# Reordered steps, four places for raw weights, and two fold copies on another engine in a fused recurrence and Fourier-mixing kernel

## Chip, cores and metric

The kernel runs on one core of a Trainium2 chip. The metric is the time of one execution on the device in microseconds; lower is better. Five engines run side by side, each in the order in which its instructions were written: TensorE (PE, matrix products), VectorE (DVE), ScalarE (ACT), GpSimd (POOL) and SyncE (SP, which here only issues DMAs). They wait for one another by semaphores.

## What is computed

Two blocks follow one another. The first is a gated recurrence over 768 tokens, for 4 batches and 8 heads of dimension 48:

```
f = 1 / (1 + exp(-f_logit))
for t in range(S):
    state = f[:, :, t, :, None] * state + einsum('bhd,bhe->bhde', k[:, :, t], v[:, :, t])
    y[:, :, t] = einsum('bhd,bhde->bhe', q[:, :, t], state)
```

The heads are laid side by side, which gives x of 768 tokens by 384 channels for each batch. The second block mixes it by a two-dimensional Fourier transform and then runs a two-layer network:

```
mixed = real(fft(fft(x, axis=1), axis=2))
u  = x + mixed
un = (u - mean(u)) / sqrt(var(u) + 1e-6)
out = u + relu(un @ w_ch1) @ w_ch2        # 384 -> 1536 -> 384
```

## The kernel before

Work is cut into steps, and a hand-written list of words, `ORDER`, says in which order the steps are issued. A loop walks over the list and calls a generator or a function for each word. Nothing else sets the order: each engine gets its share of every step in the order of the list, and waits where an operand is not there yet.

**Attention units.** A number (0 to 15) is the next step of one unit; a unit is two heads of one batch, so units 0 to 3 make batch 0. In the text, 1.7 is step 7 of unit 1. The steps: 0, ScalarE turns the logits into log gates (L372, L373); 1, VectorE scans them (L379, L380); 2, ScalarE takes three exponentials (L383 to L387); 3, VectorE multiplies them into q and k (L391, L392); 4, PE makes the scores inside blocks of 64 tokens (L400); 5, VectorE masks them (L404); 6, PE makes the first half of the values and the scores across blocks, ScalarE copies these; 7, PE makes the rest of the values (L559) and the state products (L599); 8, VectorE scans the states (L607); 9, PE adds what the states give (L616), ScalarE empties the accumulator `y` in five copies; 10, PE turns the result into token rows (L636) and ScalarE copies them to `x`; 11, the fold, on VectorE, which adds and subtracts token tiles in mirror pairs for the transform (L663 to L669); 12, for the last two units of a batch, a second fold along the channels (L678 to L687). `y` exists once, so the values of one unit start after the copies of the unit before.

`K3` turns the keys of unit 3 (PE, then a ScalarE copy). `L3fk` has SP issue the loads of f and k of unit 3; q, k and f are 344 KB each, in two DMAs, v is 369 KB. The homes of f, k and q are few and are reused by later units, so a load can wait until an earlier unit has read its own.

**Weights.** The weights come as 64-bit words. `r` fetches one raw block of 393 KB (24 in all), `R` three, and `C` makes 32-bit floats of one block (ScalarE L281, VectorE L283 and L284, POOL L285). Raw blocks take turns in a pool of three buffers, so a fetch waits for the block three before it. `V` and `c` read weight blocks a second time, late in the run, to judge their size (L344); `M` decides from that whether everything has to be done again in another way, which doesn't happen with these inputs.

**Mixing and network.** `F1` is the next step of batch 1's transform: four products with tables into `z`, which ScalarE copies, and three mixing steps, each of which adds to two token tiles of `x`. `H1` is the next step of the normalisation of batch 1: moments of a tile, or a tile normalised by VectorE (L779), turned by PE (L782) and copied by ScalarE. `P1` is the next step of the network for batch 1, which takes pairs of token tiles. For batches 1 to 3 the first layer is a scheme of 15 products (`PRODUCTS`, L840), each with sums of tokens made by VectorE before it (L814), an evacuation by ScalarE (L847) or an addition by VectorE (L849), and a ReLU by ScalarE (L851). The second layer is a scheme of seven products (L894) into two accumulators. `B` makes sums of weights for the first scheme, `W` for the second.

**Pairs and stores.** `PAIRS` names the pairs of token tiles, `LAST_PAIRS` those of the last batch: (2, 5), (1, 3), (0, 4). A tile's rows go back to the output as soon as they are finished: tiles 1, 2, 3 and 5 by an indirect DMA on POOL's queue (L692), tile 0 by one DMA and tile 4 by three on SP's queue. The last pair of the last batch, (0, 4), has a branch of its own (L915 to L933): its products come in another order, so that after the last one only half a tile (192 columns) is left to add and store.

**Spare products.** `D` calls `busy()`, which issues eight products of 128 by 128 bf16 constants into an unused corner of `y`. They compute nothing that is used. The list holds 21 `D`.

`T` loads the tables, `S` sorts them (POOL), `Z` and `I` set constants (POOL), and `i` loads an identity matrix.

Of the kernel before, what the change touches and what calls it, by code (L numbers as in the profile page):

```python
# [27 lines left out]
    "L0f Z I 0 L0q L2q D D L1f L0k D 0 D 0 i D 1 L2f 2 0 D D D L0v 0 L1k K0 D 0 0 D L1q 0 1 D r 1 L3fk D "  # L28
    "D D L1v 2 0 L2k 1 D r r D 1 2 1 3 3 0 C K1 1 2 0 C 1 L3q 2 1 3 C L2v 2 r K2 L4fk 3 L3v L5fk 1 2 1 D "
    "T 2 0 4 3 D C S 1 2 5 3 D 2 3 2 4 K3 3 D L5qv L4qv 5 4 3 2 3 L6fk 3 2 3 5 R 3 F0 F0 4 6 F0 L6qv F0 C "  # L30
    "C 4 C 5 4 F0 r 5 K4 D 4 H0 r 4 r H0 C H0 4 C r L7fk F0 6 4 P0 C P0 6 5 P0 7 C F0 4 P0 r K5 r C L7qv "
    "P0 P0 r r 5 6 C 6 5 r 7 C 5 P0 r 7 P0 C P0 5 r 7 K6 C P0 6 C P0 r r 6 7 7 C C 6 6 r 5 P0 P0 r C 6 r "
    "C K7 H0 r P0 C 7 L9fk 6 H0 L8fk P0 L8qv C B 7 C H0 B 7 B 9 9 B 8 P0 8 9 P0 P0 L9qv P0 6 8 P0 P0 P0 "
    "P0 9 P0 P0 8 7 B 9 K9 P0 P0 5 P0 B 6 P0 P0 B P0 7 W P0 9 B H0 9 8 9 B H0 7 P0 L11fk P0 11 P0 P0 P0 "
    "P0 P0 P0 4 11 9 P0 P0 P0 P0 P0 9 B P0 P0 P0 P0 7 L11qv P0 8 11 F1 P0 8 K8 F1 F1 11 F1 L10fk 8 8 10 "
    "F1 P0 8 11 H1 L10qv B 10 F1 P0 B P0 B P0 11 P0 P0 10 B 10 H1 P0 10 K10 P0 B 10 H1 10 K11 L12fk P1 P1 "
    "P1 P1 P1 P1 P1 B P1 P1 P1 P1 P0 P1 P1 P1 F1 P1 P1 H1 10 9 12 10 P1 P1 12 10 9 8 P1 P1 P1 L12qv 12 11 "
    "12 12 8 11 P1 L13fk 12 11 H1 10 H1 P1 11 H1 H1 P1 P1 P1 P1 P1 P1 P1 P1 P1 P1 P1 P1 P1 P1 10 P1 P1 12 "
    "K12 10 P1 12 L13qv 11 P1 L14fk 12 11 P1 13 13 12 P1 P1 11 P1 14 13 P1 F2 P1 14 F2 P1 P1 P1 P1 P1 P1 "
    "P1 P1 P1 P1 P1 14 P1 13 F2 P1 L14qv 14 P1 F2 13 13 F2 13 K13 F2 14 13 H2 F2 13 14 H2 P1 L15fk P1 P1 "  # L40
    "15 15 13 K14 P1 P1 L15qv P1 14 P1 H2 14 H2 H2 P2 14 P2 P2 15 P2 P2 P1 P2 P2 P2 15 V P2 P2 P2 P2 P2 "
    "P2 P2 13 14 15 H2 H2 15 K15 15 13 12 15 14 P2 15 14 15 P2 P2 V c 12 P2 15 P2 c V 14 P2 15 P2 H2 P2 "
    "P2 P2 15 c F3 F3 F3 P2 V V P2 P2 P2 c V c P2 V P2 c P2 P2 V P2 F3 c P2 P2 V F3 F3 P2 F3 H3 P2 P2 P2 "
    "P2 P2 P2 P2 P2 H3 P2 V P2 P2 V H3 P2 P2 c P2 P2 V P2 c c P2 P2 P2 V P2 P2 P2 P2 P2 P2 P2 c P2 P2 V "
    "P2 H3 V P2 P2 H3 P3 H3 c P3 P3 c P3 P3 c P3 P3 P3 P3 c V P3 V P2 P3 P3 P3 c P3 P3 P3 P3 P3 V V P3 P3 "
    "P3 P3 V H3 P3 P3 P3 H3 P3 c P3 P3 P3 P3 c P3 P3 P3 P3 P3 V P3 P3 P3 P3 P3 P3 P3 P3 c P3 P3 P3 P3 P3 "
    "V P3 P3 c P3 V P3 c P3 c P3 P3 V c c P3 P3 P3 P3 P3 P3 M P3 P3 P3 P3 P3 P3 P3 P3"
# [32 lines left out]
LAST_PAIRS = ((2, 5), (1, 3), (0, 4))  # L80
# [3 lines left out]
def kernel(  # L84
# [81 lines left out]
    small = fixed([128, 2 * NF], "small")  # L166

# [21 lines left out]
    def busy():  # L189

        for _ in range(8):
            nc.tensor.matmul(spare, lhsT=bound[:, :C], rhs=bound[:, :C], start=not started, stop=True,  # L192
                             skip_group_check=True)
            started.append(True)
# [111 lines left out]
    def words(i):  # L306
        _, src, cols = blocks_of[i]
        raw = pr.tile([128, 2, 3, DM // 2], U32, tag="raw", name=f"raw{i}").rearrange("p a b n -> p (a b n)")
# [380 lines left out]
    def store(b, c, rows):  # L689
# [7 lines left out]
        for i, j, o in {0: [(0, C, 0)], 4: [(0, 1, 3 * QS), (1, 16, HS + 1), (16, C, HS + 16)]}[c]:  # L697
            nc.sync.dma_start(out=out[b, o:o + j - i], in_=rows[i:j])
# [155 lines left out]
    def projected(b, x, again=False):  # L854
# [5 lines left out]
        for j, (c, d) in enumerate(PAIRS if b < B - 1 else LAST_PAIRS):  # L860
            if again:
                for _ in range((3, 3, 2)[j]):
                    next(behind[b], None)
# [250 lines left out]
```

## Time and profile before

| | |
|---|---|
| runs before | 524.42, 525.7, 527.98 us, median 525.7 |
| profiled execution | 527.98 us, of which the profile's span is 526.3 |
| PE busy | 494.9 us, 94% of the span |
| VectorE busy | 378.3 us, 72% |
| ScalarE busy | 218.4 us, 42% |
| POOL busy | 58.8 us, 11% |
| mean granted PE clock | 0.974 of full speed |
| first product of batch 0's transform | 59.54 us |
| last product ends | 519.43 us |
| DMA | 48.15 MB, 91 GB/s on average |

Busy time is the time in which an engine has at least one instruction running; the span is from the first instruction of the profiled execution to the last. Some 1.7 us of the execution lie outside the span. A busy share over the whole span is an average of stages with different limits, so it has to be read together with the view that cuts the span into stretches. In the profile a group of instructions is named by the line of the kernel, the engine and the operation; "idle before" tells how long the engine stood still just before an instruction and what released it.

### The profile page before, as it was taken

The numbers are of one execution on the slowest core, as the hardware profiler recorded it, in microseconds if no ns is written. First come the engines' busy times: TensorE is split into PE (matmuls) and PEld (weight loads), VectorE is DVE, ScalarE is ACT, GpSimd is POOL, SyncE is SP. The second block draws the span as 40 slices with busy tenths as digits, with TensorE's granted clock in tenths as the row PEclk, the third lists the DMA queues.
The fourth block names the chain that finished last, engine by engine and source line by source line (L and its number), as shares of the span: only waits on it lengthen the run. The fifth ranks groups of instructions, "written<-read, shape, count | busy, mean of one in ns | idle before, by whom it ended". The sixth has DMA issues, their size and how long they took to land.

```text
span 526.3 us, 13807 instructions
## 1 busy us (share of the span) xinstructions
PE 494.9 (94%) x5854; PEld 453.4 (86%) x5854; DVE 378.3 (72%) x746; ACT 218.4 (42%) x520; POOL 58.8 (11%) x85
## 2 busy tenths in 40 slices
PE   5878599999999999999999999999999999999994
PEld 4757388866899889999999999999999999999994
DVE  3598989989955368688588776779776667465571
ACT  5567368656331542453435523550431404031220
POOL 3045033551001000000001000000001000010100
PEclk9789699999999999999999999999999999999998
DMA  8957837575010230103212012120610312220200
GB/s 222 268 147 206 210 109 214 161 221 158 6 55 30 68 97 17 54 21 114 77 55 84 1 55 72 46 63 23 206 43 15 107 47 81 83 91 8 84 11 27
DMA packets 20650, 48.15 MB, mean 91 GB/s; under 512 B 3426, under 2 KB 6179, under 8 KB 20579
## 3 DMA queue, kind: packets, MB, share of 16 engines
q1 hardware_dynamic: 19474, 43.63, 29.5%
q0 software_dynamic: 1104, 3.54, 1.8%
q8 instruction: 48, 0.79, 0.6%
q14 instruction: 24, 0.19, 0.1%
HBM read 42.44 MB, written 4.72 MB: 90 GB/s over the span
## 4 chain that ended last, share of the span: by engine, by line
PE 87%; DVE 6%; issue 2%; ACT 2%; DMA 1%; POOL 0%; SPq 0%; DVEq 0%; ACTq 0%
PE ub L840 23%; PE fx L894 16%; PE fz L894 11%; PE up L871 9%; PE z L724 5%; PE y L559 4%; PE mix L743 3%; PE y L616 2%; PE sc L400 2%; PE ds L599 2%; PE po L880 2%; PE yt L636 2%; PE pt L782 1%; PE st L538 1%; PE y L192 1%
## 5 line engine op out<-in xcount | busy, mean ns | idle before, releaser
L849 DVE TENSOR_TENSOR h<-h,ub 128x512 f32<-128x512 f32 x81 | 55.2, 687 | 33.5 <-PE ub L840 24.5
L692 POOL DMA_INDIRECT out_dram<-x,place x16 | 16.4, 1024 | 357.6 <-DVE x L944 224.3
L847 ACT ACTIVATE h<-ub 128x512 f32<-128x512 f32 x54 | 31.9, 591 | 42.3 <-PE ub L840 42.3
L871 PE MATMUL up<-unT,w 128*128 128x256 f32 x216 | 49.4, 382 | 0.0
L840 PE MATMUL ub<-wide,w 128*128 128x128 f32 x360 | 45.0, 276 | 2.3 <-DVE wide L814 2.3
L894 PE MATMUL fx<-block,h 128*128 128x192 f32 x264 | 46.9, 328 | 0.0
L894 PE MATMUL fx<-w,h 128*128 128x192 f32 x264 | 45.5, 327 | 0.0
L840 PEld LDWEIGHTS ub<-wide,w 128*128 128x128 f32 x360 | 42.4, 192 | 3.4 <-PE pt L782 1.3
L871 PEld LDWEIGHTS up<-unT,w 128*128 128x128 f32 x216 | 40.1, 190 | 5.9 <-ACT h L873 0.4
L851 ACT ACTIVATE h<-h 128x512 f32<-128x512 f32 x45 | 28.4, 631 | 38.1 <-DVE h L849 37.7
L894 PEld LDWEIGHTS fx<-block,h 128*128 128x128 f32 x264 | 43.2, 190 | 0.5 <-DVE x L911 0.2
L894 PEld LDWEIGHTS fx<-w,h 128*128 128x128 f32 x264 | 42.7, 190 | 0.4 <-issue 0.2
L285 POOL TENSOR_TENSOR w<-w,raw 128x384 uint32<-128x384 uint32 x24 | 29.4, 1228 | 72.3 <-DVE w L284 39.1
L840 PE MATMUL ub<-unT,w 128*128 128x128 f32 x288 | 37.0, 275 | 0.0
L840 PEld LDWEIGHTS ub<-unT,w 128*128 128x128 f32 x288 | 34.6, 192 | 0.0
L783 ACT COPY unT<-pt 128x384 f32<-128x384 f32 x24 | 11.4, 484 | 46.8 <-PE pt L782 46.6
L840 PE MATMUL ub<-unT,wide 128*128 128x128 f32 x216 | 29.1, 278 | 0.0
L840 PE MATMUL ub<-wide 128*128 128x128 f32 x216 | 28.6, 275 | 0.1
L873 ACT ACTIVATE h<-up 128x256 f32<-128x256 f32 x36 | 13.9, 385 | 33.6 <-PE up L871 22.0
L840 PEld LDWEIGHTS ub<-unT,wide 128*128 128x128 f32 x216 | 26.4, 192 | 0.5
L840 PEld LDWEIGHTS ub<-wide 128*128 128x128 f32 x216 | 26.3, 192 | 0.3 <-PE ub L840 0.3
L379 DVE TENSOR_TENSOR_SCAN W<-g,bound 112x768 f32<-112x768 f32 x12 | 21.0, 1747 | 6.7 <-ACT g L373 6.7
(194 smaller groups left out, 1000.1 us busy)
## 6 DMA issues: line engine op xcount, KB each, us to landing
raw<-in_w_ch_dram SPq DMA_DIRECT2D x24, 384.0 KB, 5.1
v<-in_v_dram SPq DMA_DIRECT2D x16, 288.0 KB
k<-in_w_ch_dram SPq DMA_DIRECT2D x12, 384.0 KB, 3.4
g<-in_w_ch_dram SPq DMA_DIRECT2D x12, 384.0 KB, 3.3
k<-in_qkf_dram SPq DMA_DIRECT2D x14, 288.0 KB
g<-in_qkf_dram SPq DMA_DIRECT2D x12, 288.0 KB, 3.5
q<-in_qkf_dram SPq DMA_DIRECT2D x12, 288.0 KB, 3.3
wide<-in_qkf_dram SPq DMA_DIRECT2D x10, 288.0 KB, 4.7
```

Of the source, the lines that this page charges most:

```text
L285: nc.gpsimd.tensor_tensor(bits, bits, lo, ALU.add)
L379: nc.vector.tensor_tensor_scan(W, g, bound[:R], 0.0, ALU.add, ALU.min)
L559: nc.tensor.matmul(y[FILL[g], c // 3, c % 3 * C + t.start:c % 3 * C + t.stop], lhsT=vals[rows, o:o + (64 if g == 0 else D)], rhs=weights, ...
L692: nc.gpsimd.indirect_dma_start(out=out.rearrange("b s d -> (b s) d"), out_offset=bass.IndirectOffsetOnAxis(ap=place[:, b, i:i + 1], axis=0 ...
L724: nc.tensor.matmul(z[:, cols], lhsT=src[:, j, lo:hi], rhs=tab[:, t, T % 2, cols], start=(i == 0), stop=(i == len(parts) - 1), skip_group_c ...
L743: nc.tensor.matmul(mix[:, o], lhsT=zz[:rows_of[T], T, PLACES[c]], rhs=cd[:rows_of[T], T, :NQ - odd], start=(i == 0), stop=(i == 1))
L840: nc.tensor.matmul(chains[chain][:, m * 128:(m + 1) * 128], lhsT=block(w)[:, m * 128:(m + 1) * 128], rhs=tokens(a), start=(new and m == 0) ...
L847: nc.scalar.activation(out, got, kind, scale=1.0 if how == "=+" else -1.0)
L849: nc.vector.tensor_tensor(out, out, got, ALU.add if how == "+" else ALU.subtract)
L851: nc.scalar.activation(out, out, AF.Relu)
L871: nc.tensor.matmul(pp[:, :256], lhsT=w1[:, kt, m * 128:(m + 1) * 128], rhs=unT[:, kt], start=(kt == 0), stop=(kt == 2))
L894: nc.tensor.matmul(out, lhsT=h[:, m], rhs=blocks[i][:, m], start=(start and m == 0), stop=(m == H - 1), skip_group_check=True)
```

## The change

Six things change.

1. `busy()` issues two products instead of eight. The same constants are read as 32-bit floats, 128 of them. A 32-bit product is recorded by the profile as two products with two weight loads.
2. The raw weight blocks get a fixed tile, `ring`, with four places used in turn, instead of a pool of three. The three temporary blocks of `combine()` lie in it too.
3. In the fold, the two copies between VectorE's additions and subtractions (L667 and L668) are issued on ScalarE.
4. The pairs of the last batch are (2, 5), (1, 4), (3, 0), normalised in that order.
5. The branch for the last pair goes; the last pair runs as every other pair does. Tile 0 of the last batch is stored on ScalarE's DMA queue.
6. `ORDER` is another list, of the same 720 words: every word occurs as often as before.

```diff
-    "L0f Z I 0 L0q L2q D D L1f L0k D 0 D 0 i D 1 L2f 2 0 D D D L0v 0 L1k K0 D 0 0 D L1q 0 1 D r 1 L3fk D "
-    "D D L1v 2 0 L2k 1 D r r D 1 2 1 3 3 0 C K1 1 2 0 C 1 L3q 2 1 3 C L2v 2 r K2 L4fk 3 L3v L5fk 1 2 1 D "
-    "T 2 0 4 3 D C S 1 2 5 3 D 2 3 2 4 K3 3 D L5qv L4qv 5 4 3 2 3 L6fk 3 2 3 5 R 3 F0 F0 4 6 F0 L6qv F0 C "
-    "C 4 C 5 4 F0 r 5 K4 D 4 H0 r 4 r H0 C H0 4 C r L7fk F0 6 4 P0 C P0 6 5 P0 7 C F0 4 P0 r K5 r C L7qv "
...
+    "L2q Z I L0f D D L1f i 0 D L2f L0k D L0q D D L1k 1 D L0v D D 0 D 2 L3q D 0 0 1 D 0 K0 1 0 D 0 L1q 1 r "
+    "L3fk D 1 L2v L2k 3 2 C 1 0 L1v r 0 D 2 D 0 K1 2 K2 3 1 1 L5fk L3v 2 L4fk C 1 T 2 3 3 1 r 5 1 D r D 5 "
+    "2 4 3 S 1 2 D L6fk 2 3 4 2 0 K3 3 L5qv 0 D 3 3 2 3 C 2 3 3 2 5 3 D 4 F0 6 5 F0 L4qv F0 R F0 C L6qv 4 "
+    "C 4 C 4 F0 4 L7fk K4 4 C H0 H0 4 K5 4 H0 6 L7qv 6 F0 r P0 r 6 C r r 5 5 4 C L8fk P0 7 P0 P0 r 5 6 C "
...
-LAST_PAIRS = ((2, 5), (1, 3), (0, 4))
+LAST_PAIRS = ((2, 5), (1, 4), (3, 0))
...
+    ring = fixed([128, 3 * NF // 2 * HD], "ring")
...
-        for _ in range(8):
-            nc.tensor.matmul(spare, lhsT=bound[:, :C], rhs=bound[:, :C], start=not started, stop=True,
-                             skip_group_check=True)
+        words = bound.bitcast(F32)[:, :C]
+        for _ in range(2):
+            nc.tensor.matmul(spare, lhsT=words, rhs=words, start=not started, stop=True, skip_group_check=True)
...
-        raw = pr.tile([128, 2, 3, DM // 2], U32, tag="raw", name=f"raw{i}").rearrange("p a b n -> p (a b n)")
-        raw = raw[:, :768].rearrange("p (n w) -> p n w", w=2)
+        raw = ring[:, i % 4 * 2 * DM:(i % 4 + 1) * 2 * DM].bitcast(U32).rearrange("p (n w) -> p n w", w=2)
...
-        nc.vector.tensor_copy(f[:, 1:7:5], f[:, 0:8:7])
-        nc.vector.tensor_copy(f[0:1, 0], f[0:1, 2])
+        nc.scalar.copy(f[:, 1:7:5], f[:, 0:8:7])
+        nc.scalar.copy(f[0:1, 0], f[0:1, 2])
         tt(f[0:1, 2:7:4], x[0:1, 0:2, ch], x[0:1, 3:5, ch], ALU.subtract)
...
-            nc.sync.dma_start(out=out[b, o:o + j - i], in_=rows[i:j])
+            queue = nc.scalar if (b, c) == (B - 1, 0) else nc.sync
+            queue.dma_start(out=out[b, o:o + j - i], in_=rows[i:j])
...
-            if (b, c) == (B - 1, 0):
-                nc.sync.dma_start(out=out[b, :C, :HD], in_=c1)
...
-                tt(c2, Z, c2, ALU.add)
-                nc.sync.dma_start(out=out[b, :C, HD:], in_=c2)
```

In the new list unit 2's q is the first load, ahead of unit 0's f; all three first steps of units 0, 1 and 2 stand ahead of unit 0's exponentials (0.2); twelve `D` stand ahead of unit 0's scores (0.4), and the runs of `D` behind them are shorter; all 21 `D` stand ahead of batch 0's transform, where before one stood behind it. The late part of the list, from batch 1's network on, has the same words in a similar order.

## The prediction

> **What bounds the kernel now.** The page comes first. TensorE (PE) is busy for 494.9 of 526.3 us, so the digits by slice must say where it is not.
>
> ```profile
> PE 494.9 (94%) x5854; PEld 453.4 (86%) x5854; DVE 378.3 (72%) x746; ACT 218.4 (42%) x520; POOL 58.8 (11%) x85
> ...
> PE   5878599999999999999999999999999999999994
> ...
> DVE  3598989989955368688588776779776667465571
> ...
> PEclk9789699999999999999999999999999999999998
> ```
>
> Each digit is 13.2 us. PE is below 9 in the first five slices and in the last, and its clock is down in the same early slices. Next comes the table of stretches.
>
> ```profile
> 15.00:20.00 5.00, 2.68 (x72) 2.12 (x69) 2.34 (x4) 3.85 (x6) 0.00 (x0) 0.77 1.05 274
> 20.00:25.00 5.00, 5.00 (x54) 4.80 (x52) 2.57 (x3) 2.17 (x4) 0.00 (x0) 0.55 1.03 290
> 25.00:30.00 5.00, 4.35 (x161) 3.72 (x164) 3.97 (x6) 2.98 (x10) 0.04 (x1) 1.00 0.28 63
> ...
> 26.00:58.00 32.00, 22.63 (x595) 18.67 (x587) 29.38 (x53) 21.51 (x53) 13.35 (x20) 0.85 0.74 189
> 58.00:145.00 87.00, 83.97 (x1094) 66.07 (x1095) 79.55 (x134) 51.09 (x130) 25.73 (x21) 0.96 0.52 148
> 145.00:519.00 374.00, 370.71 (x3822) 352.62 (x3820) 257.85 (x548) 130.56 (x314) 14.87 (x15) 1.00 0.20 60
> ```
>
> The columns are PE, weight loads, VectorE (DVE), ScalarE (ACT), POOL, the granted clock, the DMA share and GB/s. There are three stages. From 0 to 26 us everything waits, behind loads (DMA share 1.05) and a PE at half clock. From 26 to 58 VectorE is busy 29.4 of 32 us and is the bound. From 58 PE is: 84.0 of 87, then 370.7 of 374. So PE's work after the first transform is fixed, and the end moves with the moment that F0 (batch 0's transform) starts, with PE idle time after it (1.5 us of the 3.0 up to 145, and 3.3), and with the last 7 us. The timeline shows how VectorE lost the first stage and what releases F0:
>
> ```profile
> 18.33 0.48 PE L559 MATMUL y<-at,v 64*48 64x64 f32 x7 [2.25 <-issue]
> 20.11 4.93 PE L192 MATMUL y<-bound 128*128 128x128 bf16 x48
> ...
> 20.23 0.76 DVE L607 TENSOR_TENSOR_SCAN stt<-ds,te 112x288 f32<-112x288 f32 x1 [2.82 <-PE ds L599]
> ...
> 25.96 1.04 DVE L404 COPY_PREDICATED at<-causal,sc 128x768 f32<-128x768 uint32 x1 [3.08 <-PE sc L400]
> ...
> 58.98 0.46 DVE L681 TENSOR_TENSOR se<-xs 128x285 f32<-128x285 f32 x1
> ...
> 59.54 2.85 PE L724 MATMUL z<-tab,se 128*95 128x385 f32 x6 [4.38 <-issue]
> ```
>
> PE stopped 2.25 us on nothing that the profile names, in the middle of unit 0's values; the trace has a 16 KB instruction packet running from 15.73 to 16.93, so I read it as code arriving late. Then six D steps (48 spare products) ran at half clock, 4.93 us, ahead of unit 1's scores, and VectorE waited 2.82 and 3.08 us. At the end of the stage PE waited 4.38 us for `se` (58.98 + 0.46 = 59.44), and F0 began at 59.54.
>
> **The front, old sum.** I add VectorE's rows by step: scan 1.92, the two products 1.94, mask 1.03, state scan 0.75, fold 2.47, second fold 1.0 or 3.2, a weight block 1.1. Up to F0 the old list holds 44.8 us of it, 2.3 of that after `se`: 42.5 before it. Idle before VectorE's steps: 6.48 + 0.97 + 1.20 + 2.82 + 3.08 = 14.55, then 1.35 + 0.20. 42.5 + 16.1 = 58.6 against 59.4; the 0.8 more is rows stretched here (1.27 for a weight row of 0.56, 0.90 for a copy of 0.20). I keep it as 0.9.
>
> **The front, new list.** Loads in the old trace land at some 255 GB/s, 1.35 us for each of 344 KB, the first at 4.5, and 2.13 MB at 11.56. L2q now stands ahead of L0f, so f0 lands at 5.9 and unit 0's two ScalarE passes (1.9) end at 7.8: VectorE starts 1.3 later than 6.48. Its scan ends at 9.75. ScalarE now has units 1 and 2's passes ahead of unit 0's exponentials: 7.8 to 9.7, and 9.7 to 11.6 (f2, 1.44 MB, is in by 8.8), so the first exponential ends at 12.45, where it was 9.38. q0 completes 2.13 MB, 11.5. VectorE waits 2.7 there; idle so far is 10.5. From there it has work queued: 0.3, 1.1, 0.5 at 16.3, 1.3 at 17.95 (q1 in at 17.0), 2.1, a weight block, 1.5, 0.8 at 23.85, 2.3 at 24.6 (k2 in at 24.0), 3.1. The twelve D steps ahead of unit 0's scores last at most 12 x 0.82 = 9.8 us (half clock, 4.93/6 each) from 4.6, that is to 14.4, when those scores are ready anyway. No later useful step has more than two D directly before it. Later waits by the same walk: 1.2 for unit 1's states (its values wait until 27.4 for ScalarE to empty `y`), 1.35 for f5's passes, 0.9 for unit 2's rows.
>
> VectorE's work to F0 is 43.7 us by the same rows (one weight block fewer), less 2.3 after `se`, less four times the two copies (0.26 + 0.24): 39.4. **The copies on ScalarE** don't free VectorE as much as they take off it: L669 writes rows that the copies read and write, so it must wait for both. Rows nearest to them are ScalarE's copies of 265 and 180 ns; with two handovers of about 0.1 that is 0.7 of waiting for 0.5 of work, if ScalarE is free. Lower bound -0.5 (hidden wholly); upper bound 2.0, behind one product of 0.89 and one activation of 0.63. I take 0.7, since up to F0 ScalarE is busy only 21.5 of 32 us. Sum: 39.4 + 0.9 + 10.5 + 1.2 + 1.35 + 0.9 + 4 x 0.7 = 57.0, so F0 at 57.1: **-2.5 us**. Bounds: -4.5, if q2 costs f0 only its two issue slots (0.93) and the later waits vanish; +1.5, if loads lag by a further 1 us (the old trace's lag grows from 1.15 to 2.2 us by 19.06), the code stall comes back on the path (2.25 less 1.2 of slack) and two later waits grow by 1 each. PE's useful work before F0 is the same in both lists, so the shift passes on whole.
>
> **D in float words.** Eight bf16 products become two f32 ones, each recorded as two. The row ub<-wide gives 0.89 us for eight such records at full clock, so a D is 0.45; bf16 measured 0.53 to 0.62. Cost nothing before F0, where D fills idle time; uncovered it would be 21 x 0.45. The one D that stood behind F0 (before unit 4's values) is now ahead: **-0.45**. PE instructions of a D fall from 16 records to 8, 168 in all, some 13% of the first 1,280; that makes late code less likely, and I book nothing for it.
>
> **Raw words in four places.** In the old trace SP stands at a raw load from 23.5 to 31.5 until a place is free, all loads behind it: hence 63 GB/s above. With four places and the new list SP first stands at L5fk, for unit 1's last read, about 28.3. VectorE's queue hides that: 0 in the sum. After F0, raw data made VectorE wait 0.76 at 109 and 0.96 at 116.6; near the end of the weights the new list is tighter (the last fetch five steps ahead of its use, thirteen before), so 0, from -1 to +1.5.
>
> **Later folds and pair changes.** Twelve folds follow F0, some with ScalarE queued behind PE's products. VectorE has 7.5 us spare in 58 to 145 and over 100 after. Where PE needs VectorE two products later, a wait of 2.0 less 2 x 0.89 leaves PE 0.22 us each, at most 2.6 in all; the lower end is -0.6, half of the two gaps of 0.69 and 0.57 at 100.7 and 117.5. I take **+0.8**, a little under the middle, for the spare time. At the change of pairs (0.52, 0.61, 0.94 us) both lists put the same filler within two steps: 0, from -1 to +1.
>
> **The end.**
>
> ```profile
> 517.52 0.56 DVE L927 TENSOR_TENSOR x<-fx,x 128x384 f32<-128x384 f32 x1 [1.59 <-PE fx L894]
> ...
> 519.47 0.36 DVE L930 TENSOR_TENSOR x<-fz,x 128x192 f32<-128x192 f32 x1 [1.39 <-PE fz L894]
> 519.86 0.36 SPq L931 DMA_DIRECT2D out_dram<-x  x1
> ```
>
> The branch for the last pair goes. After the last product there is now the 384-column addition, 0.56 for 0.36, then one issue on ScalarE's queue, which has nothing before it: **+0.2**. The indirect store of tile 3 is ready one product (1.95) earlier and takes POOL 1.02, so it lies under that. Four issues on SP become none.
>
> **Sum.** -2.5 - 0.45 + 0.8 + 0.2 = -1.95. The profiled execution took 527.98, 2.3 above the median of 525.7, so it becomes 526.0 and the median **523.7**.
>
> [...] PE's clock in the trace is 1.0 from 7.4 to 17.7, half to 24.5, full to 34.7, half to 41.6, and half again from 55.2 to 65.5. In the stretch 14.26 to 17.68 PE was busy for 1.8 of 3.4 us, and the clock fell at its end: half a stretch of idling was enough. The new list leaves PE some 5 us idle just before F0 with one D in it, so the clock falls there again. F0's 28 products at half clock took 8.4 us where a later batch takes 5.2: 3.1 us lost now and, in my sum, lost again. [...]
>
> **Rivals.** *VectorE waits for ScalarE in the folds.* L669 then waits 2.0, not 0.7, because ScalarE takes its queue in order. Four folds ahead of F0 cost 4 x 1.3 = 5.2 more: F0 at 62.3, sum +3.25, **528.9**, slower than before. It decides once the wait passes 0.7 + 1.95/4 = 1.2 us. For it: ScalarE is the engine between PE and VectorE all through these units. Against it: its 10 us of idle time in 26 to 58. *The front's gain is given back*, in lost cover behind F0: folds at 2.6 instead of 0.8 and pair changes at their +1 give 2.8 more, **526.5**. For it: PE's own gaps there are short because VectorE is just in time. Against it: VectorE's share drops. *The clock stays up.* If spare products spread singly keep every window over half full, F0's 3.1 us and some 1.5 of the units' slow steps go too: **519.1**. Against it: the 5 us gap before F0. *The edits do nothing that can be seen*, since the front's order is bound by loads: 525.7; it lies between the others and shares the second one's chance.
>
> **How the numbers follow.** Forecast 0.48 (own range 521 to 526), gain given back or no effect 0.24, folds waiting 0.16, clock kept 0.12. Leaving out the tails of the outer two gives 518.0 to 530.5. One per cent, 5.3 us, is about what a measurement of this kernel can tell from no change: faster than 520.4 takes the clock's case and a little of the forecast's edge, 0.14; slower than 531.0 takes half of the folds' case, 0.09; within, 0.77.
>
> **What would show it.** VectorE's first scan at 7.8, not 6.48; its idle time before the 16th microsecond larger, and no wait of 2.8 or 3.1 between 17 and 26; F0's first product near 57; L669 some 0.7 us after the end of L666; full DMA between 26 and 28 us; the clock half around F0; PE continuous after it, ending near 517.3. F0 at 59.5 or later, or PE gaps of over 8 us after F0, would prove it wrong.

## The result, and the profile after

The changed kernel takes 531.29 us (median of 20 runs, 528.69 to 534.44); the kernel before took 525.92 in the same rounds. The ratio is 1.0096, with a 95% interval of 1.0074 to 1.0118: about 1% slower, where 523.7 was forecast. The profiled execution took 533.2 us, its span is 531.5, 5.2 longer than before.

The page of the changed kernel, its busy times and its slices of 13.3 us:

```profile
PE 494.9 (93%) x5770; PEld 453.6 (85%) x5770; DVE 371.5 (70%) x714; ACT 226.6 (43%) x552; POOL 57.0 (11%) x85
...
PE   5787599899999999999999999999999999999994
```

PE is busy for exactly as long as before, 494.9 us, so the 5.2 us are PE idle time. The digits differ from before in slices two to four and in the eighth, which was a 9 and is an 8. The table of stretches (PE, weight loads, VectorE, ScalarE, POOL, clock, DMA share, GB/s) says which stages hold them:

```profile
20.00:25.00 5.00, 3.95 (x132) 3.54 (x136) 4.92 (x8) 4.28 (x7) 1.02 (x1) 1.00 1.04 231
25.00:30.00 5.00, 3.75 (x116) 3.00 (x116) 4.05 (x6) 3.41 (x11) 0.00 (x0) 1.00 0.27 71
26.00:58.00 32.00, 21.98 (x562) 18.60 (x560) 21.05 (x37) 18.14 (x52) 8.81 (x18) 0.87 0.79 212
58.00:145.00 87.00, 81.17 (x1080) 63.86 (x1081) 78.46 (x126) 56.59 (x142) 25.49 (x22) 0.95 0.50 143
145.00:519.00 374.00, 368.61 (x3795) 349.63 (x3794) 255.98 (x532) 135.87 (x334) 15.90 (x14) 1.00 0.20 60
```

The start went as forecast: from 20 to 25 us VectorE is busy for 4.92 of 5, where it was busy for 2.57, and the waits of 2.82 and 3.08 us near 20 and 26 are gone. Then the gain goes. From 26 to 58 VectorE is busy for 21.05 of 32 us, before for 29.38: it is no longer the engine that works through, it waits. From 58 to 145 PE works 2.80 us less than before, from 145 on 2.10 less. The timeline of the changed kernel shows the waits of the first stage (start, duration, engine, line; the bracket is the idle time before and what ended it):

```profile
39.28 0.36 DVE L666 TENSOR_TENSOR eo<-eo 128x192 f32<-128x192 f32 x1
40.20 0.84 ACT L372 ACTIVATE g<-g 112x768 f32<-112x768 f32 x1 [2.60 <-DMA g<-in_qkf_dram]
...
41.91 0.34 ACT L667 COPY eo<-eo 128x192 f32<-128x192 f32 x1
42.28 0.27 ACT L668 COPY eo<-eo 1x96 f32<-1x96 f32 x1
42.58 0.34 DVE L669 TENSOR_TENSOR eo<-x 1x192 f32<-1x192 f32 x1 [2.94 <-ACT eo L668]
...
50.06 0.35 DVE L669 TENSOR_TENSOR eo<-x 1x192 f32<-1x192 f32 x1 [1.08 <-ACT eo L668]
55.44 0.73 DVE L669 TENSOR_TENSOR eo<-x 1x192 f32<-1x192 f32 x1 [0.81 <-ACT eo L668]
58.41 0.35 DVE L669 TENSOR_TENSOR eo<-x 1x192 f32<-1x192 f32 x1 [0.72 <-ACT eo L668]
...
60.55 2.85 PE L725 MATMUL z<-tab,se 128*95 128x385 f32 x6 [4.93 <-issue]
```

VectorE finished L666 at 39.64 and could not go on before 42.58. The two copies take 0.34 and 0.27 us, but ScalarE stood until 40.20 at unit 4's first step (4.0), for unit 4's f, did its two passes, and only then came to the copies. The four folds ahead of F0 wait 2.94 + 1.08 + 0.81 + 0.72 = 5.55 us. F0 starts at 60.55, 1.0 later than before. Behind it PE idles 8.66 us up to its last product, before 4.77: that is 1.0 + 3.9 of the 5.2. PE's busy time behind F0 grew by another 0.4 (455.5 us, before 455.1). The end, from PE's last product to the end of the span, is as long as before (6.80 for 6.82):

```profile
523.40 0.97 POOL L692 DMA_INDIRECT out_dram<-x,place  x1 [28.72 <-DVE x L925]
524.72 0.56 DVE L929 TENSOR_TENSOR x<-fx,x 128x384 f32<-128x384 f32 x1 [1.59 <-PE fx L895]
526.55 0.38 ACTq L699 DMA_DIRECT2D out_dram<-x  x1
```

### The profile page after: what moved, and what is told of

Its sections match the earlier page's. It is cut to its first block, busy times and chain, and to the rows that moved or that the text cites. A ratio compares the mean times of both kernels' runs of the same rounds, so it can differ in the third digit from the quotient of the medians.

```text
span 531.5 us, 13640 instructions
## 1 busy us (share of the span) xinstructions
PE 494.9 (93%) x5770; PEld 453.6 (85%) x5770; DVE 371.5 (70%) x714; ACT 226.6 (43%) x552; POOL 57.0 (11%) x85
## 4 chain that ended last, share of the span: by engine, by line
PE 79%; DVE 8%; DMA 6%; ACT 3%; issue 2%; SPq 1%; DVEq 0%; ACTq 0%
PE ub L841 23%; PE fx L895 16%; PE fz L895 12%; PE up L872 5%; PE z L725 5%; PE y L559 3%; PE po L881 3%; PE mix L744 2%; DMA g<-in_qkf_dram 2%; DMA wide<-in_qkf_dram 2%; PE y L616 2%; PE ds L599 2%; PE pt L783 2%; DVE w L285 1%; PE yt L636 1%
## 5 line engine op out<-in xcount | busy, mean ns | idle before, releaser
L692 POOL DMA_INDIRECT out_dram<-x,place x16 | 18.4, 1148 | 384.7 <-DVE x L925 252.3
L895 PE MATMUL fx<-ring,h 128*128 128x192 f32 x264 | 46.6, 327 | 0.0
L872 PEld LDWEIGHTS up<-unT,w 128*128 128x128 f32 x216 | 40.2, 190 | 6.3 <-ACT h L874 0.8
L895 PEld LDWEIGHTS fx<-ring,h 128*128 128x128 f32 x264 | 43.3, 190 | 0.1
L286 POOL TENSOR_TENSOR w<-w,ring 128x384 uint32<-128x384 uint32 x24 | 27.0, 1131 | 70.3 <-ACT ring L282 30.2
L770 ACT ACTIVATE rstd<-mv,eps 128x1 f32<-128x1 f32 (+1 forms) x20 | 5.9, 294 | 43.1 <-DVE mv L767 43.1
```

What stands on the lines that cost most here:

```text
L286: nc.gpsimd.tensor_tensor(bits, bits, lo, ALU.add)
L692: nc.gpsimd.indirect_dma_start(out=out.rearrange("b s d -> (b s) d"), out_offset=bass.IndirectOffsetOnAxis(ap=place[:, b, i:i + 1], axis=0 ...
L872: nc.tensor.matmul(pp[:, :256], lhsT=w1[:, kt, m * 128:(m + 1) * 128], rhs=unT[:, kt], start=(kt == 0), stop=(kt == 2))
L895: nc.tensor.matmul(out, lhsT=h[:, m], rhs=blocks[i][:, m], start=(start and m == 0), stop=(m == H - 1), skip_group_check=True)
```

## The experiments

All eighteen in one table. F0, PE's idle time from F0 to its last product, and the tail (last product to the end of the span) are from each kernel's one profiled execution; ratios are to the kernel before in the same rounds (median 525.8 to 526.5).

| run | what it is | median us | ratio, 95% interval | profiled us | F0 at | PE idle behind F0 | tail |
|---|---|---|---|---|---|---|---|
| before | | 526.2 | | 527.98 | 59.54 | 4.77 | 6.82 |
| after | | 531.29 | 1.0096 [1.0074, 1.0118] | 533.2 | 60.55 | 8.66 | 6.80 |
| e1 | after, copies on VectorE | 529.3 | 1.0058 [1.0036, 1.0081] | 529.75 | 55.74 | 8.60 | 8.87 |
| e2 | before, copies on ScalarE | 535.4 | 1.0172 [1.0132, 1.0213] | 534.21 | 59.70 | 9.36 | 6.90 |
| e3 | e2, float `D`, `ring` | 537.9 | 1.0210 [1.0170, 1.0251] | 538.5 | 62.67 | 9.48 | 6.60 |
| e4 | e1, bf16 `D` | 533.3 | 1.0135 [1.0098, 1.0171] | 531.3 | 57.91 | 7.98 | 8.96 |
| f1 | new front, old rest | 525.5 | 0.9976 [0.9951, 1.0000] | 524.55 | 55.81 | 5.49 | 6.52 |
| f2 | old front, new rest | 528.6 | 1.0061 [1.0029, 1.0093] | 527.62 | 56.73 | 7.86 | 6.74 |
| f3 | before, float `D` | 528.0 | 1.0027 [1.0000, 1.0053] | 529.12 | 60.20 | 6.05 | 6.75 |
| f4 | e1, last store on SP | 528.9 | 1.0044 [1.0018, 1.0071] | 529.53 | 57.47 | 8.58 | 8.16 |
| g1 | f1, bf16 `D` | 529.1 | 1.0071 [1.0040, 1.0103] | 528.49 | 60.30 | 6.53 | 6.52 |
| g2 | after, 4.0 moved | 526.6 | 1.0008 [0.9989, 1.0027] | 528.54 | 57.19 | 7.77 | 6.89 |
| g3 | e1, two words moved | 530.0 | 1.0086 [1.0058, 1.0113] | 528.11 | 55.11 | 8.07 | 9.24 |
| g4 | f1, f0 loaded first | 525.4 | 0.9989 [0.9960, 1.0018] | 523.98 | 55.26 | 5.81 | 6.50 |
| h1 | f1, four half float products | 542.9 | 1.0320 [1.0285, 1.0356] | 541.27 | 73.45 | 4.96 | 6.60 |
| h2 | g2, copies on VectorE | 527.4 | 1.0024 [1.0003, 1.0045] | 526.98 | 55.12 | 8.12 | 8.70 |
| h3 | f1, nine more `D` ahead of F0 | 528.3 | 1.0036 [1.0013, 1.0060] | 528.39 | 56.66 | 8.77 | 6.56 |
| h4 | g4, nine more `D` ahead of F0 | 529.0 | 1.0043 [1.0019, 1.0067] | 527.93 | 55.36 | 9.57 | 6.52 |
| j1 | g4, 4.0 moved | 525.5 | 0.9995 [0.9966, 1.0024] | 525.63 | 56.25 | 7.53 | 6.56 |
| j2 | f1, four bf16 products | 524.9 | 0.9968 [0.9943, 0.9993] | 524.95 | 55.90 | 7.08 | 6.54 |

Two warnings for the columns that come from a single execution. The profiled execution (column "profiled us") lies up to 2 us off its kernel's median. And e1 and f4, which are the same program up to the last store, have F0 1.7 us apart, so a difference of F0 below some 2 us tells nothing. The kernel before varies with its clock: of its 135 runs in the rounds of the experiments, the 50 with a mean granted clock of 0.983 or more have a median of 524.8 us, the 45 with 0.977 or less one of 527.9. Its profiled execution, with 0.974, is of the second kind.

### The copies (e1 to e3) and the list without them (e4)

The edit of e1, undone in e2 and e3 on the old list; e4 is e1 with the eight bf16 products of before.

```diff
-        nc.scalar.copy(f[:, 1:7:5], f[:, 0:8:7])
-        nc.scalar.copy(f[0:1, 0], f[0:1, 2])
+        nc.vector.tensor_copy(f[:, 1:7:5], f[:, 0:8:7])
+        nc.vector.tensor_copy(f[0:1, 0], f[0:1, 2])
```

> The changed kernel with the two fold copies back on VectorE, all else changed. In the changed kernel VectorE waits for ScalarE's copy before L669 16 times, 15.6 us in all, 5.55 us of it in the four folds ahead of F0; PE starts F0 at 60.55 and idles 3.9 us between F0 and its last product beyond what the old kernel does. Theory 1 (the fold's wait): the copies cost VectorE 0.5 us each time, so F0 comes 5.55 - 2.0 = 3.5 us earlier, near 57, and some of the later PE idle time goes; the time falls to 526 to 528. Theory 2 (the list): the new order itself holds up the units and opens PE gaps; F0 stays at 60 or later and the time stays within 1 us of 531.3.

> The old kernel with the two fold copies moved to ScalarE, nothing else. Theory 1: each fold gains a wait of at least 0.35 + 0.27 us plus two handovers, more where ScalarE has other work queued; four folds ahead of F0 cost 1 to 3 us and later ones some PE cover: 527.5 to 530. Theory 2: VectorE loses some tenths per fold, hidden behind PE: 525.5 to 526.8.

> The old list, pairs and ending, with the three other edits: float spare products, four places for raw words, copies on ScalarE. Theory 1: like the copies alone, 527.5 to 530. Theory 2: like the old kernel, 525 to 527. If float spare products or the four places matter by themselves, this differs from the copies alone by over 1 us; by the old profile I expect less.

> The new list with its four places, its pairs and its ending, but copies on VectorE and bf16 spare products. Theory 1: the list alone costs nothing or gains a little, 525 to 528, F0 near 57 to 58. Theory 2: 530 or more, F0 at 60 or later. Against the kernel with the copies back it shows what float words do in this list: 168 PE instructions more before F0, so late code could stop PE again for 1 to 2 us; otherwise the same within 0.5 us.

With the copies back on VectorE the changed kernel's F0 starts 4.8 us earlier, and PE ends 5.5 earlier (519.16), but the median falls by 2.0 only. Part of the difference is that the changed kernel's profiled execution took 1.9 more than its median; another part is the end, where e1's profile shows this row:

```profile
520.95 2.89 ACTq L699 DMA_DIRECT2D out_dram<-x  x1
```

The same issue on the same queue took 0.38 us in the profile of the changed kernel; the tail is 2.1 longer. That the long issue makes the long tail is not shown: in f4 the issue takes 0.34 us, and the tail is 8.16.

In the old list the copies alone cost 9 us. F0 stays where it was, so the loss lies behind it: in the profile 4.6 us more of PE idle time and 1.4 more of PE busy time. The timeline of e2:

```profile
133.78 0.36 DVE L666 TENSOR_TENSOR eo<-eo 128x192 f32<-128x192 f32 x1
...
138.93 0.39 ACT L873 ACTIVATE h<-up 128x256 f32<-128x256 f32 x1 [0.91 <-PE up L871]
139.21 0.34 ACT L667 COPY eo<-eo 128x192 f32<-128x192 f32 x1
...
139.89 0.34 DVE L669 TENSOR_TENSOR eo<-x 1x192 f32<-1x192 f32 x1 [5.75 <-ACT eo L668]
...
149.74 0.86 PE L782 MATMUL pt<-ident,un 128*128 128x128 f32 x3 [3.78 <-DVE un L779]
```

ScalarE has three ReLUs of the network and the copies of `yT` and `kT` ahead of the fold's copies, and each group of them waits for a product; so VectorE stands for 5.75 us behind PE's own pace. What VectorE should have made meanwhile (L779) is late, PE stands 3.78 us at 146, and its clock halves for 3.4 us (the three products of L782 at 149.74 take 0.86 us, such rows of the kernel before 0.49 to 0.55). The cause is the same as in the changed kernel, ScalarE's order, with another blocker: there a load, here products. e3's longest front wait was 3.41, its total 24.2 us in 16 folds (e2 20.6, the changed kernel 15.6). What e4 told, 4 us more than e1 for bf16 words, was not understood at this point.

### The list in halves (f1, f2), the float form (f3), the last store (f4)

```diff
 f1, against before
-ORDER: old words 1 to 121, then the old rest
+ORDER: new words 1 to 123, then the old rest without its first D and first 5   (float D, ring)
 f2, against after
-ORDER: new words 1 to 123, then the new rest
+ORDER: old words 1 to 121, then a 5 and the new rest, with one D behind K4   (copies on VectorE, bf16 D)
 f3, against before
-            8 products of 128 by 128 bf16
+            2 products of 128 by 128 float words
 f4, against e1
-            queue = nc.scalar if (b, c) == (B - 1, 0) else nc.sync
+            queue = nc.sync
```

> The new list up to the start of batch 0's transform and a little beyond (its first 123 words), the old list from there on (less one D and one step of unit 5, which the new front already holds); float spare products, four places, copies on VectorE, old pairs and old ending. Theory 1 (front gains, rest loses): with the copies back F0 came at 55.7 against 59.5 of the old kernel, but PE idled 8.6 us from F0 to its last product against 4.8, and the tail was 8.9 against 6.8. Then this one has F0 at 55.5 to 58, PE idle time after F0 near 4.8, a tail of 6.8: 522 to 524.5, faster than both. Theory 2 (a gain in front is always given back, because weights or later units arrive no sooner): F0 early all the same, PE idle time after F0 8 us or more, 525.5 to 528.

> The other splice: old list up to batch 0's transform, new list from there on, with the new pairs and ending, four places, copies on VectorE, bf16 spare products. Theory 1: F0 near 59.5, PE idle time after F0 near 8.6, tail 6.8 to 8.9: 529.5 to 532.5. Theory 2: the later gaps came from the earlier start, so they close here: PE idle time after F0 near 5, 525.5 to 528.

> The old kernel with the float spare products alone. In the new list without the copies, float words were worth 533.3 - 529.3 = 4 us; the two kernels with the old list and the copies differ the other way, 535.4 without and 537.9 with float words and four places. If fewer PE instructions make code arrive in time (the old profile's stop of 2.25 us at 16 us), F0 comes 1 to 2 us earlier: 523.5 to 525.5. If float words do nothing by themselves: 525.5 to 527. If they weigh less for PE's clock, the half-clock stretches before F0 grow beyond 18 us: 527 to 530.

> The changed kernel with copies on VectorE and the last store on SP's queue in place of ScalarE's. With the copies back and the store on ScalarE's queue the profile shows 8.9 us from PE's last product to the end, of which the issue itself took 2.9, and 529.3 in all. Theory 1 (the first and only DMA of ScalarE's queue is slow to issue): the issue takes 0.4, the tail is 6.8 to 7.2, 527 to 528. Theory 2 (it waits for the indirect store ahead of it on any queue): the tail stays near 8.9, 529 to 530.

The two halves pull apart. The new front gains 3.7 us at F0 in its profile and 0.2% in the median; the new rest loses: PE idles 7.86 us behind F0, 5.49 with the old rest. Here the spare products differ too; e1 and f1 have the same front, form and place of the copies and differ only in the rest, the pairs and the ending: 8.60 against 5.49, and 529.3 against 525.5 us. The larger gaps that only the new rest has are, in e1, 0.91 near 69 and 1.38 near 97 us (PE waits for `ao`, which ScalarE copies only after an inverse square root, L770, for which it stands waiting for VectorE's moments), 0.72 near 109, and 0.50 and 0.85 at 328 and 366; f2 has 0.46 in place of the first.

f2 missed its expectation at F0. Its first 121 words are the old ones, so F0 was expected near 59.5, and it came at 56.73. Where the kernel before waited 2.82 and 3.08 us, f2's VectorE waits less:

```profile
17.69 0.76 DVE L607 TENSOR_TENSOR_SCAN stt<-ds,te 112x288 f32<-112x288 f32 x1 [0.55 <-PE ds L599]
...
21.54 1.01 DVE L404 COPY_PREDICATED at<-causal,sc 128x768 f32<-128x768 uint32 x1 [1.20 <-PE sc L400]
```

So F0 of the kernel before is no firm base for the 3.7 us. f2 has four places for raw words, and in its execution the clock stayed whole from 9.5 to 43.7 us, where the kernel before had half from 17.7 to 24.5; which of the two took the waits away is not separated.

The last store gains nothing on SP: it is issued in 0.34 us, and the tail is 8.16.

### One word (g2), two words (g3), the loads (g4), bf16 words in the new front (g1)

```diff
 g2, against after
-    2 4 3 S 1 2 D
+    2 3 S 1 4 2 D
 g3, against e1
-    F0 4 L7fk K4 ... r r 5 5 4 C ... 7 F0 P0 r r 6 C 7
+    F0 5 4 L7fk K4 ... r r 5 4 C ... 7 6 F0 P0 r r C 7
 g4, against f1
-    L2q Z I L0f D D
+    L0f Z I L2q D D
```

> The new front with the old rest of the list, and the spare products back as eight bf16 ones of 128 by 128 per D. The float form alone, in the old list, gave 528.0 against 526.3. Theory one, the form of the spare products is worth some microseconds whatever the list: with bf16 words this kernel differs from its float twin (525.6) by 1.5 us or more, 524 if float words cost what they did in the old list, 528 to 530 if they help in the new front as the two kernels with the whole new list suggested (529.3 with float words, 533.3 with bf16). Theory two, the form is neutral and those differences come from the clock and from what PE's code fetch meets: 525 to 526.5, F0 within 0.5 us of 55.8 at the same granted clock.

> The changed kernel with one word moved: unit 4's first step (4.0, two ScalarE passes over f4) comes after the fold of unit 1 (1.11) and not ahead of it, so that ScalarE does not stand at f4's load with the fold's copies behind it. Theory, ScalarE's order is what costs the folds: the first wait of L669 falls from 2.94 to 0.7 to 1.1 us, F0's first product comes 1.5 to 2.5 us earlier, 529 to 529.8 against 531.3, about what taking the copies back to VectorE gives (529.3). Rival, the load is what bounds: the wait at L669 goes but VectorE waits as long at a later step, F0 stays near 60.5 and the time near 531.

> The changed kernel with the fold's copies on VectorE, and two words moved: unit 5's state scan (5.4 in the list's late part of the first network) earlier, between two steps of batch 0's transform, and a step of unit 6 ahead of the transform's next step. Theory, PE's gaps of 0.91 us near 69 and 1.39 us near 99 are there because ScalarE stands at the square roots (L770) for VectorE's moments while a copy that PE needs is queued behind: with the steps moved both gaps close, PE idles some 6.3 us behind F0 in place of 8.6, and the time is 527 to 527.8 against 529.3. Rival, the gaps only move, since VectorE has the same work in this stretch: PE idles 8 us or more behind F0 and the time is 529 or more.

> The new front with the old rest of the list, and unit 0's f as the first load, unit 2's q as the third, as the old list has them in this order. Theory, the order of the first loads sets when VectorE starts and nothing bound by other loads follows: the first scan starts near 6.5 and not at 8.4, F0's first product comes 0.5 to 1.5 us earlier than 55.8, 524 to 525 us. Rival, later loads and ScalarE's passes set the pace of the front: F0 stays within 0.4 of 55.8 and the time at 525 to 526.

g2 decides the main question. One step moved by three words takes the changed kernel from 531.3 to 526.6 us. Its timeline:

```profile
39.58 0.35 ACT L667 COPY eo<-eo 128x192 f32<-128x192 f32 x1 [2.08 <-DVE eo L666]
39.96 0.27 ACT L668 COPY eo<-eo 1x96 f32<-1x96 f32 x1
40.26 0.35 DVE L669 TENSOR_TENSOR eo<-x 1x192 f32<-1x192 f32 x1 [0.72 <-ACT eo L668]
41.00 0.84 ACT L372 ACTIVATE g<-g 112x768 f32<-112x768 f32 x1 [0.78 <-DMA g<-in_qkf_dram]
...
57.19 2.85 PE L725 MATMUL z<-tab,se 128*95 128x385 f32 x6 [4.92 <-issue]
```

The copies go first, f4 comes when it comes, and all four waits ahead of F0 are 0.72 us. F0 starts at 57.19.

g3 is a miss. The gap of 0.91 closed, but 0.84 came at 66.7, 1.49 at 90.3 (PE waits for `yT`, ScalarE's copies) and the tail was 9.24: the rival, gaps that only move. g4 moved the first scan from 8.0 to 6.5 us and F0 by 0.55, less than e1 and f4 differ by, and the time by nothing that can be told (the intervals of f1 and g4 overlap). g1 came out 3.6 us above its float twin f1 by the medians, and the two intervals lie 0.4% apart. Its profile has one stall that f1 lacks:

```profile
38.19 0.37 PE L599 MATMUL ds<-v,kT 128*64 128x48 f32 x5
41.78 0.43 PE L599 MATMUL ds<-v,kT 128*64 128x48 f32 x9 [3.21 <-issue]
```

PE stood for 3.21 us in the middle of a row of like products on nothing that the profile names. One 16 KB packet of the instruction queue ran from 38.97 to 40.13, inside the stall. Such a packet alone makes no stall: in j2 seven of them run ahead of F0, and PE stands at none of them for more than 0.15 us.

### Form or number (h1, j2), the copies again (h2), the clock (h3, h4), the parts together (j1)

```diff
 h1, against f1
-            2 products of 128 columns, float words
+            4 products of 64 columns, float words
 j2, against f1
-            2 products of 128 columns, float words
+            4 products of 128 columns, bf16
 h2, against g2: the copies on VectorE, as in e1
 h3, against f1 (h4 the same, against g4)
-    D 4 F0 6 5 F0
+    D 4 D D D D D D D D D F0 6 5 F0
 j1, against g4
-    2 4 3 S 1 2 D
+    2 3 S 1 4 2 D
```

> The new front with the old rest of the list, and a spare product step of four float products of half the columns (64) in place of two of 128: as many PE records as the eight bf16 products have (16 with the weight loads), in the float form. With two float products this list took 525.6, with eight bf16 ones 529.1, whose profile shows PE standing 3.21 us near 38.6 on nothing that it names. Theory one, the number of PE instructions ahead of the transform is what counts, through code that arrives late: 528 to 530 and a stall of 2 us or more without a named releaser before F0. Theory two, the form of the words is what counts: 525 to 526.5 and no such stall.

> The changed kernel with unit 4's first step behind unit 1's fold (526.6) and the fold's copies on VectorE as well. Theory, what is left of the copies' price once ScalarE's order is mended is the handover, 0.72 of waiting for 0.5 of work in each of the four folds ahead of F0, and some later folds: F0 about 1 us earlier than 57.2 and 525 to 526. Rival one, the copies then cost nothing at the end: 526.3 to 527. Rival two, the moved word only helps where copies stand behind it, and the last store's issue is what keeps the kernel with copies on VectorE at 529.3: 528.5 to 529.5.

> The new front with the old rest of the list (525.6), and nine more spare steps ahead of the transform's first product, some 4.1 us at full clock inside the 5.0 us for which PE waits there. Theory, the clock falls because that window is half idle: with it filled the clock stays whole through F0, the 5.7 us at half clock behind F0 go, 2.8 us are gained, 522.5 to 523. Rival, the clock falls anyway or the spare steps run at half clock and end behind the transform's tables: 525 to 527.5, F0 up to 2 us later.

> As the kernel with nine more spare steps ahead of the transform, and unit 0's f as the first load. By the theories of the two parts 2.8 us from the clock and 0.2 to 0.5 from the load: 522 to 522.8, faster than both kernels. Rival: the earlier start moves the windows and the clock still falls once in the front, 524 to 525.5.

> The new front with unit 0's f as the first load and unit 4's first step behind unit 1's fold, the old rest of the list, float spare products, the fold's copies on VectorE, the old last pairs and their branch: the parts that helped, put together. The kernel with the first load swapped took 525.4. Theory, the moved step also lets ScalarE copy unit 2's rows without standing at f4's load, as the profile of the changed kernel with that step and the copies on VectorE showed (first product of the first network at 73.0 us, against 74.2 here before): 523.5 to 524.8, faster than both kernels by 0.2 to 0.5 per cent of the kernel before. Rival, without the copies nothing stands behind the load: 525 to 526.

> The new front with the old rest of the list, and a spare product step of four bf16 products of 128 by 128: 8 PE records a step as the float form has, in bf16, and about half the time (0.28 us at full clock). The float form took 525.6, eight bf16 products 529.1 with a stall of 3.21 us that nothing named explains. Theory one, the number of PE instructions counts: the stall is gone or below 1 us and the time 524.5 to 526.5. Theory two, the form of the words counts: 528 to 530 with a stall of 2 us or more in the front. Rival, shorter spare steps let the clock fall more: half clock ahead of F0 for over 12 us, where the float form had 8.0, and 526.5 to 528.

h1 told nothing of its question: a float product of half the columns was no shorter (from one record to the next 0.213 us at half clock, as with all columns in f1), and the clock, which rose at 10.3 us in f1, rose only at 37.75. So the first twelve `D` took 20.75 us, 1.73 each, and unit 0's scores started at 25.3, in f1 at 14.1. The spare work itself became the bound.

j2 answers it. As many PE records per `D` as the float form, in bf16: 524.9 us, no unnamed stall over 0.15 us before the wait for F0's tables, and the only interval that lies wholly below the kernel before (0.9968, 0.9943 to 0.9993). So the bf16 form itself costs nothing that can be told. Beside that, fewer records are not enough: f3 has them too, in the old list, and stands 2.62 us near 25.1 on nothing named. Where such a stall falls changes with the number and the order of PE's instructions (near 16 us in the kernel before, 25.1 in f3, 38.6 in g1); that it is late code is an inference from the instruction packet of 16,384 bytes beside it, and no run shows it.

h2 puts the remaining price of the copies at nothing that the end can tell: F0 is 2.1 us earlier than in g2, PE ends 3.4 earlier, and the tail (8.70 for 6.89) and the spread between runs take it back: 527.4 against 526.6. The expected 525 to 526 was wrong.

With the changed kernel, e1 and g2 this makes a square: step 4.0 early, copies on ScalarE 531.3 and on VectorE 529.3; step 4.0 late, 526.6 and 527.4. The copies cost 2.0 us while 4.0 stands ahead of them, and nothing once it is moved. Moving 4.0 is worth 4.7 us with the copies on ScalarE and 1.9 without; what the 1.9 are was not looked for. The intervals of the 4.7 lie apart; those of the 2.0 and of the 1.9 overlap a little.

h3 and h4 are the surprise. Nine more `D` filled PE's gap ahead of F0 (5.00 to 0.99 us), the clock stayed whole through F0's four products, and the time rose by 2.7 us, above what either expectation had. The half clock was not taken away but moved: it came from 68.83 to 75.65 us, 6.8 us behind F0 where f1 had 5.7. The timeline of h3, PE, POOL (and below it the POOL row of f1) and VectorE in turn:

```profile
63.57 0.93 PE L400 MATMUL sc<-q,g 48*64 48x64 f32 x48 [0.97 <-DVE g L392]
...
69.30 1.01 PE L538 MATMUL st<-ident,g 112*128 112x112 f32 x4 [2.01 <-DVE at L404]
```

```profile
63.93 2.40 POOL L286 TENSOR_TENSOR w<-w,ring 128x384 uint32<-128x384 uint32 x2 [11.94 <-ACT ring L282]
```

```profile
65.38 3.94 POOL L286 TENSOR_TENSOR w<-w,ring 128x384 uint32<-128x384 uint32 x4 [14.23 <-ACT ring L282]
```

```profile
64.30 1.18 DVE L284 TENSOR_SCALAR w<-ring 128x384 uint32<-128x384 uint32 x1
65.51 1.25 DVE L285 SCALAR_TENSOR_TENSOR w<-ring,w 128x384 uint32<-128x384 uint32 x1
```

PE at full clock came to the next units' scores sooner and waited there for VectorE, 0.97 and 2.01 us (4.05 in all up to the first network, 0.60 in f1). ScalarE emptied `z` sooner, so POOL's part of the weight blocks (L286) began at 63.93 where it began at 65.38, and now ran beside VectorE's part of the next blocks: rows of 0.35 and 0.56 us took 1.18 and 1.25. The first product of the first network came at 78.86, in f1 at 75.02. The row of L285 that had begun at 63.82, just ahead of POOL's, took 0.56, the row of L284 that began at 66.68, between two of POOL's, 0.35, and the row of L285 at 67.06, beside POOL's next, 1.25 again. Why a row that begins beside POOL's takes so long is not shown.

j1 shows that the parts do not add up: 525.5, not below f1, g4 or j2.

## Why the prediction was wrong

**The step that failed first: the price of the copies, "0.7 of waiting for 0.5 of work, if ScalarE is free".** The 0.7 was right, to 0.02: it is 0.72 in all four folds of g2. The condition was not checked fold by fold. I took it from ScalarE's share of a stretch (21.5 of 32 us busy); but an engine that waits is not free. At the first fold ScalarE had stood idle for 2.60 us, blocked by a step that the new list puts ahead of the copies. The rival had the mechanism (L669 waits because ScalarE takes its queue in order) and a price of 2.0 in each of four folds; the waits were 2.94, 1.08, 0.81 and 0.72. Only the first passed the stated deciding point of 1.2, and the sum of the four, 5.55 against the 2.8 of my sum, is past 4 x 1.2 = 4.8. Its 528.9 was below what came, since it too took the rest of the list at nothing. By the medians this step is worth 2.0 of the 7.6 us that the forecast missed (e1).

**The step behind it: "VectorE's queue hides that: 0 in the sum", for the raw places.** SP stood at unit 5's loads, as forecast (from 21.76 to 28.88 us; "about 28.3"), so the full DMA that I listed for 26 to 28 did not come: 71 GB/s from 25 to 30, before 63. I asked only whether VectorE would run dry. The load queued behind was f4; it was issued at 32.50, landed at 40.2, and ScalarE stood at it:

```profile
32.50 0.58 SPq L213 DMA_DIRECT2D g<-in_qkf_dram  x1
```

With step 4.0 moved behind the fold the time is 526.6, 4.7 less; this is shown by g2. F0 then starts at 57.19, forecast 57.1: that it is so close is luck, since e1 and f4, with the same front, have F0 1.7 us apart. That f4 is late because SP stood is read from the issue times and was not tried by itself; 7.7 us lie between its issue and its landing, as much as SP stood (7.1).

**The rest of the list, "so 0, from -1 to +1.5", and the folds' +0.8.** Behind F0 I had 4.77 + 0.8 = 5.6 us of PE idle time; it is 8.66, and 7.77 in g2. The folds are not what fails: g2 and h2, with and without the copies on ScalarE, idle 7.77 and 8.12, so twelve later folds cost PE nothing here, although VectorE waits some 10 us in them (in the old list, e2, PE's idle time rose to 9.36). The term that was mis-sized is the reordering of batch 0's second half, which I priced at 0 by the raw weights alone. Its 0.91, 1.39 and 0.72 are read as coming from ScalarE and VectorE steps that changed places; g3 moved two of these and only moved the gaps, so which steps it takes stays open. f1 and f2, which swap the halves, put the rest of the list at 2.4 us of idle time, e1 and f1 at 3.1, or 3.7 us of the time with the ending. My own refutation line, gaps of over 8 us behind F0, was met.

**What held.** First exponential and product: 12.49 us, forecast 12.45. No waits of 2.8 and 3.1 between 17 and 26. The clock half around F0. The first scan came at 8.41, not 7.8, because f0 landed at 6.5 and not 5.9.

**The base of the front's -2.5.** Without the copies' 4 x 0.2 this term is -3.3. F0 in f1, which has the copies on VectorE, is 3.7 earlier, but the median of f1 falls by 0.8 only. The sum took the waits of 2.82 and 3.08 us as part of every execution of the kernel before. They were read in one that took 2.1 us more than the median, at a clock of 0.974, and f2 waits 0.55 and 1.20 at the same two places. So the term is mis-sized by some 2.5 us by the medians; that the one profile is the reason fits these numbers and is not shown by itself.

**The clock.** I went by the stretch of the trace in which PE was busy for 1.8 of 3.4 us before the clock fell, and that held: the clock fell after windows in which PE was busy for about half the time or less (51, 53 and 55% in the kernel before, 27, 23 and 48% in the changed one). But "3.1 us lost" was no price. h3 removed the half clock at F0, got another from 68.83 on and was slower; j2 has 17.5 us of half clock ahead of F0 and the lowest median of all. In h3 VectorE sets the pace there, and PE's clock only decides where PE waits. That the clock never matters is not shown: within the kernel before, runs with the higher clock are faster by 3.1 us, and whether the clock or the waits come first is open. The rival of the clock kept up (519.1) has no run for it, but no run kept the clock whole all the way either.

**The end.** +0.2 was priced for 0.56 in place of 0.36. The profile shows 6.80 for 6.82, but that is one draw: with the same ending the tail is 6.74 to 6.89 where ScalarE's issue took 0.38 us (three profiles) and 8.70 to 9.24 where it took 2.64 to 3.04 (four). The old ending has 6.50 to 6.90. The issue also begins only after the landing of tile 3's store (526.49, then 526.55). f4's tail of 8.16 has an issue of 0.34. So the term is anything from nothing to some +2.2, and what decides stays open.

**Float words.** The -0.45 cannot be seen: PE's busy time behind F0 is 0.4 longer, not shorter. It was small beside what the number of products does, through the stalls as far as the profiles show: 3.6 us gained in the new front (f1 against g1), 4.3 by fewer bf16 products (j2), and 1.7 lost in the old list (f3, whose interval begins at 1.0000).

## What to carry to other kernels

When a short operation moves to another engine, price it by what stands ahead of it in that engine's queue at each place where it occurs, down to the load that the step ahead waits for; a low busy share says nothing, for a blocked engine is idle too. When a list is reordered, follow each late load to the step that stands at it and to what is queued behind that step on the same engine. Before paying for a higher clock, see whether the engine that gets it is the one that the others wait for. And before a wait in a profile is counted as what a change can win, see whether the profiled execution is one of the slower ones of its kernel.

## What was not expected of the hardware

- PE's clock changes on a grid of 3.41 us: from the first recorded change to the last one ahead of 100 us, the stretches at one clock last 6.83, 10.24 and 13.65 us in the kernel before, and 3.41, 6.83, 10.24 and 23.89 in the changed one. With the PE records of all 20 profiled executions merged and cut on that grid, from each one's first recorded change to 160 us: the clock fell after 52 windows, in which PE was busy for 0 to 66%; it stayed full after 714, all with 56% or more; it rose after 52, all with 81% or more; and it stayed half after 46, in seven of which PE was busy for more than 85%. So the busy share alone does not decide, and a window more than half busy can be enough for a fall: in the kernel before the clock fell after windows with 53 and 55%.
- PE can stand for 0.8 to 3.2 us between two like products with nothing named (2.25 in the kernel before, 2.62 in f3, 3.21 in g1, 0.89 in the changed kernel, none above 0.15 in j2), and changing only spare products moves or removes it. It varies between executions too: the same front stands 0.90 near 21 us in e1 and 0.19 in f4.
- One and the same DMA issue on ScalarE's queue took 0.38 us in three kernels (the changed one, f2, g2) and 2.64 to 3.04 in four (e1, e4, g3, h2).
- A float product of 64 columns took no less time than one of 128: from one record to the next 0.213 us at half clock and 0.112 at full in h1, and the same two in f1. In h1, where a row of 96 of them ran to 25.3 us, the spacing of the records shows half clock through nine windows (7.03 to 37.75 us) in which PE was busy all the time; in the other 19 executions the clock rose at 7.4 to 10.8 us, after a window that was busy for 83% or more.
